# Gated linear attention and feed-forward on one core: the recurrence's result computed transposed in quadrants of 32 columns

## The chip, the core and the metric

The kernel runs on one core of a Trainium2 chip. The metric is the device time of one execution in microseconds (us), as the median of several runs. Times inside an execution come from a profile of one further execution.

## What is computed

The reference chains a gated recurrence over 768 time steps (4 batches, 8 heads, head size 48) with a feed-forward block of 3072 tokens, 384 model columns and 2048 hidden columns. Cut to what matters:

```python
# attention: a complex gate per head and column, capped at magnitude 0.999
mag = np.sqrt(a_re * a_re + a_im * a_im)
scale = np.minimum(mag, 0.999) / (mag + 1e-06)
a_re_n, a_im_n = (a_re * scale, a_im * scale)
for t in range(S):
    S_re, S_im = (ar * S_re - ai * S_im + kv, ar * S_im + ai * S_re)   # kv = outer(k_t, v_t)
    y[:, :, t] = np.einsum('bhd,bhde->bhe', q[:, :, t], S_re)
# feed-forward on x, which is y with the heads side by side: 3072 x 384
h = x @ w_in
sp = np.maximum(h, 0.0) + np.log1p(np.exp(-np.abs(h)))
out = (h * erf(sp)) @ w_out
```

## The kernel before

Two functions stand in the file: `quotient_path`, which runs, and `product_path`, a slower fallback behind a test of value ranges at the end, which this input does not reach. All arithmetic is f32. The weights arrive in 64-bit form and are narrowed to f32 on ScalarE and VectorE in the first units (`narrow`, L676 on).

**Units and chunks.** The tokens are cut into 12 units of 256 tokens, three to a batch; each unit has two chunks (`C = 2`) of 128 tokens. In a chunk all 8 heads are treated. The recurrence is solved by chunks: the gates become cumulated magnitudes `pr` and cumulated angles `CS`, by which q and k are multiplied (`prep`, L835 and L839). That doubles the head size to 96 (cosine and sine side by side). Then, per chunk:

- `cols` (L847, L850) transposes k and q on TensorE, 4 heads to a PSUM tile `tr`, and copies them out as `kT` (ScalarE) and `qT` (VectorE).
- `state` (L870 to L879) forms `kv` = k-transposed times v for each head (96 x 48), adds the state `S` of the chunk before (`Skv`) and multiplies by the gate `w` of the chunk's last row. The first chunk of a batch has no state before it, the last one leaves none behind.
- `scores` (L858, L861) forms the 128 x 128 scores `sc` of each head, keys down the partitions and queries along the columns, and multiplies them by a triangular mask into `A`.
- `y_` (L886, L889, L894): for each head a matmul with `A` as the stationary operand (128 rows, 128 columns) and `v` as the moving one (48 columns), and, unless the chunk is the first of its batch, a second with `qT` as the stationary operand (96 rows, 128 columns) and `S` as the moving one. Both add up in PSUM tile `y`, tokens down the partitions and heads side by side. VectorE copies it to `x`.
- `xT` (L902, L903): three TensorE transposes turn `x` (128 x 384) into the PSUM tile `xt`, model columns down the partitions, and ScalarE copies it into `xT`.

The feed-forward of a unit runs one unit later, out of `xT`: `ff_in` (`hps`, L919, copied to `h` at L921), `softplus` and `erf_times_h` (L645, L948 to L951), and two units later `ff_out` (`ops`, L965).

**What sets the order.** In turn `w` the program makes a list `plan` of steps with due times between 0 and 1: the chunk steps of unit `w` (0.5 for the second chunk, plus the offsets at the end of `chunk`: `y_` at 0.36 and `xT` at 0.45), `ff_in`, `softplus` and `erf_times_h` of unit `w - 1`, `ff_out` of unit `w - 2`, gates of units ahead, the load of q, k and v of unit `w + 1` at 0.62 and of gates of unit `w + 3` at 0.72. The steps are emitted by due time, and the tile layer places the instructions on each engine's queue and adds the waits. [...]

**Buffers and queues.** All loads go through SyncE's queue (`load`, L661). v has two buffers (`bufs=2`), S two, x two. PSUM pool `ps_b` has two banks, shared by `kv`, `y`, `xt` and the gate sums.

An f32 matmul of the program appears in the trace as two MATMUL records, each with a LDWEIGHTS record (its load of the stationary operand) ahead of it: 192 matmuls with `A` (24 chunks of 8 heads) are "x384" there. A transpose of the program is one MATMUL record.

## Time and profile before

| | |
|---|---|
| median of 3 runs | 827.02 us (826.87 to 830.81) |
| the profiled execution | 830.44 us |
| its span, first to last instruction | 828.7 us |
| mean granted TensorE clock | 0.977 |
| TensorE matmuls busy (PE) | 762.6 us |
| TensorE weight loads busy (PEld) | 594.1 us |
| VectorE busy (DVE) | 550.8 us |
| ScalarE busy (ACT) | 602.3 us |

In rows of the profile, L numbers are lines of the kernel before; PE is TensorE's matmuls, PEld its weight loads, DVE VectorE, ACT ScalarE, SPq SyncE's queue of DMA issues. A row such as `y<-v,A 128*128 128x48 f32 x16` names the tiles (written from read), the rows and columns of the array, the moving operand's shape and the count. Rows of the timeline start with the start and the length in us, after merging equal neighbours. A row of groups ends with busy us, mean ns of one, and idle time before them. [...]

### The profile page before, as it was taken

How to read it: one execution, taken by the hardware profiler on the slowest of the kernel's cores; microseconds unless marked ns; L12 is line 12 of the kernel's file. 1: busy time of each engine (PE TensorE's matmuls, PEld its weight loads, DVE VectorE, ACT ScalarE, POOL GpSimd, SP SyncE). 2: the span in 40 equal slices, each digit the busy share in tenths (PEclk: the TensorE clock that was granted, in tenths of full speed). 3: DMA queues.
4: the chain of work that ended last, by engine and by line, in shares of the span. 5: the costliest groups of instructions: out<-in, count | busy, mean ns of one | idle time of the engine just before them, and what ended most of it. 6: DMA issues, size and time to landing. Idle time of an engine off the chain costs nothing.

```text
span 828.7 us, 10183 instructions
## 1 busy us (share of the span) xinstructions
PE 762.6 (92%) x3882; PEld 594.1 (72%) x3882; DVE 550.8 (66%) x875; ACT 602.3 (73%) x787; POOL 1.1 (0%) x8
## 2 busy tenths in 40 slices
PE   2446897999999999999999999999999999999996
PEld 0335695787787777777777787887777787887763
DVE  2799798866964963963973873873874774656262
ACT  7789788878876876876877867867877666566670
POOL 0000000000000000000000000000000000000000
PEclk9998699999999999999999999999999999999998
DMA  8456432211212111221212112113021010000000
GB/s 184 129 183 153 137 112 40 58 39 30 48 39 49 30 39 30 49 40 31 46 39 49 29 39 49 30 38 58 20 39 40 1 38 20 1 1 20 1 19 24
DMA packets 148034, 41.77 MB, mean 50 GB/s; under 512 B 142068, under 2 KB 145160, under 8 KB 147208
## 3 DMA queue, kind: packets, MB, share of 16 engines
q1 hardware_dynamic: 147976, 41.03, 21.7%
q8 instruction: 32, 0.52, 0.3%
q14 instruction: 26, 0.21, 0.1%
HBM read 36.24 MB, written 4.75 MB: 49 GB/s over the span
## 4 chain that ended last, share of the span: by engine, by line
PE 72%; DVE 13%; ACT 10%; issue 2%; DMA 2%; SPq 0%; DVEq 0%; ACTq 0%
PE ops L965 24%; PE hps L919 22%; PE y L886 5%; PE sc L858 5%; PE tr L847 5%; PE y L889 5%; PE kv L870 3%; ACT L644 2%; PE sum L821 2%; PE sum L754 2%; DVE yy L949 2%; DVE e L950 2%; DVE t L948 1%; ACT CS L645 1%; DVE h L951 1%
## 5 line engine op out<-in xcount | busy, mean ns | idle before, releaser
L965 PE MATMUL ops<-w_out_sb,h 128*128 128x384 f32 x768 | 269.0, 495 | 0.5 <-DVE h L951 0.5
L919 PE MATMUL hps<-xT,w_in_sb 128*128 128x256 f32 x1152 | 266.9, 384 | 1.3 <-ACT h L921 0.7
L919 PEld LDWEIGHTS hps<-xT,w_in_sb 128*128 128x128 f32 x1152 | 216.6, 192 | 34.7 <-ACT xT L903 1.0
L965 PEld LDWEIGHTS ops<-w_out_sb,h 128*128 128x128 f32 x768 | 144.5, 194 | 86.7 <-issue 4.8
L921 ACT COPY h<-hps 128x512 f32<-128x512 f32 x96 | 54.6, 580 | 113.5 <-PE hps L919 113.5
L644 ACT ACT_TABLE_LOAD x68 | 87.2, 1283 | 2.0 <-PEq L1063 0.8
L948 DVE TENSOR_TENSOR t<-z,yy 128x512 f32<-128x512 f32 x96 | 65.9, 686 | 23.8 <-ACT yy L645 22.8
L886 PE MATMUL y<-v,A 128*128 128x48 f32 x384 | 71.7, 282 | 5.8 <-DVE A L861 5.8
L645 ACT ACTIVATE e<-z 128x512 f32<-128x512 f32 x96 | 57.4, 626 | 23.1 <-DVE h L951 22.6
L886 PEld LDWEIGHTS y<-v,A 128*128 128x128 f32 x384 | 61.5, 203 | 12.2 <-ACT words L697 5.9
L950 DVE TENSOR_TENSOR e<-e,yy 128x512 f32<-128x512 f32 x96 | 64.4, 686 | 3.5
L949 DVE SCALAR_TENSOR_TENSOR yy<-t,yy 128x512 f32<-128x512 f32 x96 | 65.8, 685 | 0.7
L951 DVE SCALAR_TENSOR_TENSOR h<-e,h 128x512 f32<-128x512 f32 x96 | 64.3, 685 | 0.4
L889 PE MATMUL y<-S,qT 96*128 96x48 f32 x320 | 64.2, 283 | 0.0
L894 DVE COPY x<-y 128x384 f32<-128x384 f32 x24 | 13.4, 557 | 74.2 <-PE y L889 67.8
L858 PE MATMUL sc<-qT,kT 96*128 96x128 f32 x384 | 51.7, 284 | 0.9 <-DVE qT L850 0.9
L858 PEld LDWEIGHTS sc<-qT,kT 96*128 96x128 f32 x384 | 49.4, 197 | 3.6 <-DVE qT L850 1.2
L861 DVE TENSOR_TENSOR A<-sc,triu 128x512 f32<-128x512 f32 x48 | 32.3, 684 | 28.1 <-PE sc L858 28.1
L889 PEld LDWEIGHTS y<-S,qT 96*128 96x128 f32 x320 | 50.8, 199 | 0.0
L645 ACT ACTIVATE yy<-z 128x2048 f32<-128x2048 f32 x24 | 45.9, 1911 | 1.9 <-DVE w_out_sb L700 1.2
L645 ACT ACTIVATE z<-z 128x2048 f32<-128x2048 f32 x24 | 45.9, 1911 | 0.8
L645 ACT ACTIVATE yy<-yy 128x2048 f32<-128x2048 f32 x24 | 45.9, 1912 | 0.7
(80 smaller groups left out, 841.4 us busy)
## 6 DMA issues: line engine op xcount, KB each, us to landing
raw<-in_moe_w_in_dram SPq DMA_DIRECT2D x6, 1024.0 KB, 5.9
raw<-in_moe_w_out_dram SPq DMA_DIRECT2D x8, 768.0 KB, 5.1
ar<-in_a_re_dram SPq DMA_DIRECT2D x24, 192.0 KB, 3.5
ai<-in_a_im_dram SPq DMA_DIRECT2D x24, 192.0 KB, 3.3
q<-in_q_dram SPq DMA_DIRECT2D x24, 192.0 KB, 3.2
k<-in_k_dram SPq DMA_DIRECT2D x24, 192.0 KB, 3.1
v<-in_v_dram SPq DMA_DIRECT2D x24, 192.0 KB, 3.1
out_dram<-o SPq DMA_DIRECT2D x24, 192.0 KB, 1.9
```

Of the source, the lines that this page charges most:

```text
L644: in_order(nc.scalar.preload_act_table_set(sets[0]))
L645: in_order(nc.scalar.activation(func=func, **kw))
L858: nc.tensor.matmul(out=ps[:, j, :], lhsT=st["k", g][0:D2, j, :], rhs=st["q", g][0:D2, j, :], start=True, stop=True)
L886: nc.tensor.matmul(out=y[:, j, :], lhsT=st["A", g][:, i, :], rhs=T["v", u][:, c, j, :], start=True, stop=first)
L889: nc.tensor.matmul(out=y[:, j, :], lhsT=st["q", g][0:D2, i, :], rhs=T["S"][0:D2, j, :], start=False, stop=True)
L919: nc.tensor.matmul(out=ps[:, e, :], lhsT=w_in_sb[:, kd, f0:f0 + P], rhs=T["xT", u][:, kd, :], start=(kd == 0), stop=(kd == KD - 1))
L921: nc.scalar.copy(out=T["h", u, sl][:, i:i + 2, :], in_=ps)
L948: nc.vector.tensor_tensor(out=t, in0=z, in1=y, op=OP.mult)
L949: nc.vector.scalar_tensor_tensor(out=y, in0=t, scalar=-2.0, in1=y, op0=OP.add, op1=OP.mult)
L950: nc.vector.tensor_tensor(out=e, in0=e, in1=y, op=OP.mult)
L951: nc.vector.scalar_tensor_tensor(out=h, in0=e, scalar=1.0 / RT2, in1=h, op0=OP.add, op1=OP.mult)
L965: nc.tensor.matmul(out=ps, lhsT=T["h", u, sl][:, e, jj * P:(jj + 1) * P], rhs=w_out_sb[:, i, :], start=(i == 0), stop=(i == KF - 1))
```

## The change

The matmuls of `y_` swap their operands: `v` and `S` become stationary and `A` and `qT` moving, so that the result comes out with model columns down the partitions, which is what `xT` needs. `y_`, its copy to `x` and the three transposes go; the new `xT` (due at 0.4) runs the matmuls and the ScalarE copy stays.

[...] So the 384 model columns are cut into 12 pieces of 32 (`QUAD`), four to each of the three groups `i` of 128 partitions. Two heads (96 columns) make three pieces: the first lies in the even head, the third in the odd one, and the middle one takes 16 columns of each. v and S are therefore kept in fixed buffers of pairs of heads with 16 zero columns between them (`GAP`): a window of 32 columns that starts at column 32 holds the even head's last 16 and 16 zeros, one that starts at column 48 holds 16 zeros and the odd head's first 16. The middle piece so takes two stationary windows, one of each head, and adds them up. That makes 16 products for a chunk in place of 8, with `A` and again with `qT`: 32 matmuls (16 in the first chunk of a batch) in place of 16 (8). Each has 32 stationary columns instead of 128 and 128 moving columns instead of 48. They are emitted round the four pieces of a group: first product of each, then the second of each, and so on.

Since even and odd heads lie apart in the buffers, each of the two VectorE operations of `state` becomes two on four heads each, and each load of v becomes two. Four small memsets at the start write the zeros.

```diff
@@ -632,6 +632,22 @@
     w_out_sb = const.tile([P, KF, DM], FP, name="w_out_sb")
 
 
+    GAP, QUAD = 16, P // 4
+    PAIR = 2 * D + GAP
+    vbuf = [const.tile([P, C, H // 2, PAIR], FP, name=f"v{i}") for i in range(2)]
+    sbuf = [const.tile([P, H // 2, PAIR], FP, name=f"S{i}") for i in range(2)]
+    for t in vbuf:
+        nc.vector.memset(t[:, :, :, D:D + GAP], 0.0)
+    for t in sbuf:
+        nc.vector.memset(t[:, :, D:D + GAP], 0.0)
+
+    def side(t, e):
+
+        return t[..., e * (D + GAP):e * (D + GAP) + D]
+
     order = mybir.DependencyInfo(mybir.DependencyClass.NoSync, mybir.DependencyReason.DATA)
 
     def act(func, **kw):
@@ -670,7 +686,11 @@
         if 0 <= u < NU:
             load(ldq, "q", q, u)
             load(ldq, "k", k, u)
-            load(ldq, "v", v, u, bufs=2)
+            t = T["v", u] = vbuf[u % 2]
+            for c in range(C):
+                for e in range(2):
+                    src = rows(v, u, c).rearrange("t (h e) d -> e t h d", e=2)[e]
+                    nc.sync.dma_start(out=side(t[:, c], e), in_=src)
 
 
     def narrow(dst, src, shape, i):
@@ -868,43 +888,51 @@
             kv = ps_b.tile([P, H, D], FP, tag="b", name="kv")
             for j in range(H):
                 nc.tensor.matmul(out=kv[0:D2, j, :], lhsT=st["k"][:, j].rearrange("p u d -> p (u d)"),
-                                 rhs=T["v", u][:, c, j, :], start=True, stop=True)
-            ns = att2.tile([P, H, D], FP, tag="S", name="S")
+                                 rhs=side(T["v", u][:, c, j // 2], j % 2), start=True, stop=True)
+            ns = sbuf[(u * C + c) % 2]
             w = T["w", u, c][0:D2].unsqueeze(2).to_broadcast([D2, H, D])
             if first:
-                nc.vector.tensor_tensor(out=ns[0:D2], in0=kv[0:D2], in1=w, op=OP.mult)
+                t = kv
             else:
                 t = att1.tile([P, H, D], FP, tag="part", name="Skv", bufs=2)
-                nc.vector.tensor_tensor(out=t[0:D2], in0=kv[0:D2], in1=T["S"][0:D2], op=OP.add)
-                nc.vector.tensor_tensor(out=ns[0:D2], in0=t[0:D2], in1=w, op=OP.mult)
+                for e in range(2):
+                    nc.vector.tensor_tensor(out=t[0:D2, e::2, :], in0=kv[0:D2, e::2, :], in1=side(T["S"][0:D2], e), op=OP.add)
+            for e in range(2):
+                nc.vector.tensor_tensor(out=side(ns[0:D2], e), in0=t[0:D2, e::2, :], in1=w[:, e::2, :], op=OP.mult)
             st["S"] = ns
 
-        def y_():
-            y = ps_b.tile([P, H, D], FP, tag="b", name="y")
-            for j in range(H):
-                g, i = divmod(j, HG)
-                nc.tensor.matmul(out=y[:, j, :], lhsT=st["A", g][:, i, :], rhs=T["v", u][:, c, j, :],
-                                 start=True, stop=first)
-                if not first:
-                    nc.tensor.matmul(out=y[:, j, :], lhsT=st["q", g][0:D2, i, :], rhs=T["S"][0:D2, j, :],
-                                     start=False, stop=True)
+        def xT():
+
+            if c == 0:
+                T["xT", u] = xp.tile([P, KD, NT], FP, tag="xT", name="xT")
+            ps = ps_b.tile([P, KD, P], FP, tag="b", name="y")
+            for i in range(KD):
+                steps = []
+                for b in range(P // QUAD):
+                    pair, o = divmod((i * P + b * QUAD) // QUAD, 2 * D // QUAD)
+
+                    parts = [(0, o * QUAD)] if o * QUAD < D else []
+                    parts += [(1, o * QUAD + GAP)] if (o + 1) * QUAD > D else []
+                    todo = []
+                    for e, lo in parts:
+                        g, k_ = divmod(2 * pair + e, HG)
+                        todo.append((T["v", u][:, c, pair, lo:lo + QUAD], st["A", g][:, k_, :]))
+                        if not first:
+                            todo.append((T["S"][0:D2, pair, lo:lo + QUAD], st["q", g][0:D2, k_, :]))
+                    steps.append([(b, lhsT, rhs, n == 0, n == len(todo) - 1) for n, (lhsT, rhs) in enumerate(todo)])
+                for n in range(max(map(len, steps))):
+                    for todo in steps:
+                        if n < len(todo):
+                            b, lhsT, rhs, start, stop = todo[n]
+                            nc.tensor.matmul(out=ps[b * QUAD:(b + 1) * QUAD, i, :], lhsT=lhsT, rhs=rhs,
+                                             start=start, stop=stop)
             if not last:
                 T["S"] = st["S"]
-            x = xp.tile([P, DM], FP, tag="x", name="x")
-            nc.vector.tensor_copy(out=x, in_=y.rearrange("p h d -> p (h d)"))
-            st["x"] = x
-
-        def xT():
-            if c == 0:
-                T["xT", u] = xp.tile([P, KD, NT], FP, tag="xT", name="xT")
-            ps = ps_b.tile([P, KD, P], FP, tag="b", name="xt")
-            for i in range(KD):
-                nc.tensor.transpose(out=ps[:, i, :], in_=st["x"][:, i * P:(i + 1) * P], identity=ident)
             nc.scalar.copy(out=T["xT", u][:, :, c * P:(c + 1) * P], in_=ps)
 
         return [(0.0, prep("k", 1)), (0.03, prep("q", 0)), (0.06, cols("k", 0)), (0.09, cols("k", 1)),
                 (0.12, cols("q", 0)), (0.15, cols("q", 1)), (0.2, state), (0.25, scores(0)), (0.28, scores(1)),
-                (0.36, y_), (0.45, xT)]
+                (0.4, xT)]
 
 
     def ff_in(u, sl):
```

On TensorE's queue, here is the second chunk of unit 6 (the first unit of the third batch) in the kernel before, from the middle of its `y` block on:

```order
L889 MATMUL y<-S,qT 128x48
L886 MATMUL y<-v,A 128x48
L889 MATMUL y<-S,qT 128x48
L965 MATMUL ops<-w_out_sb,h 128x384 x4
L902 MATMUL xt<-ident,x 128x128 x3
L965 MATMUL ops<-w_out_sb,h 128x384 x4
L919 MATMUL hps<-xT,w_in_sb 128x256 x12
```

And the same chunk in the changed kernel, its whole block and what follows (v_137 and S_139 are buffers of v and S):

```order
L927 MATMUL y<-A,v_137 32x128 x4
L927 MATMUL y<-qT,S_139 32x128 x4
L927 MATMUL y<-A,v_137 32x128 x2
L927 MATMUL y<-qT,S_139 32x128 x2
L927 MATMUL y<-A,v_137 32x128 x4
L927 MATMUL y<-qT,S_139 32x128 x4
L927 MATMUL y<-A,v_137 32x128
L927 MATMUL y<-qT,S_139 32x128
L993 MATMUL ops<-w_out_sb,h 128x384 x8
L947 MATMUL hps<-xT,w_in_sb 128x256 x12
```

The part of the block ahead of these rows is one more group (x4, x4, x1, x1). In all 24 chunks the block stands in one piece, with nothing between its matmuls; the transposes are gone and the `ops` on both sides of them have closed up.

VectorE's queue around the same chunk before:

```order
L878 TENSOR_TENSOR Skv<-kv,S 96x384
L835 TENSOR_TENSOR kr<-k,pr 128x384
L879 TENSOR_TENSOR S<-Skv,w 96x384
L861 TENSOR_TENSOR A<-sc,triu 128x512 x2
L835 TENSOR_TENSOR qr<-q,pr 128x384
L969 TENSOR_SCALAR o<-ops 128x384
L894 COPY x<-y 128x384
```

And in the changed kernel:

```order
L899 TENSOR_TENSOR Skv<-kv,S_139 96x4x48 x2
L901 TENSOR_TENSOR S_140<-Skv,w 96x4x48 x2
L881 TENSOR_TENSOR A<-sc,triu 128x512 x2
L855 TENSOR_TENSOR kr<-k,pr 128x384
L855 TENSOR_TENSOR qr<-q,pr 128x384
L997 TENSOR_SCALAR o<-ops 128x384
```

Two operations of 384 columns have become four of 192, and the copy to `x` is gone.

## Prediction

> **What bounds the kernel now.** I read the page first, then the busy time by stretches, then who waits on TensorE, then the timeline of one chunk.

> ```profile
> PE 762.6 (92%) x3882; PEld 594.1 (72%) x3882; DVE 550.8 (66%) x875; ACT 602.3 (73%) x787; POOL 1.1 (0%) x8
> ...
> 0.00:150.00 150.00, 94.18 (x449) 74.52 (x449) 115.52 (x169) 122.95 (x174) 1.09 (x8) 0.92 0.50 129
> 150.00:780.00 630.00, 627.68 (x3294) 493.12 (x3294) 411.96 (x661) 458.10 (x591) 0.00 (x0) 0.99 0.17 34
> 780.00:829.00 49.00, 40.69 (x143) 26.45 (x141) 23.30 (x45) 21.25 (x24) 0.00 (x0) 0.95 0.05 18
> ...
> PE sum L754 <- DVE th L751: 18.2, 3, 6.4
> PE sum L821 <- DVE lr L793: 15.9, 1, 15.9
> ```

> The first line is of the page, the next three are stretches (length, then PE, PEld, DVE, ACT and POOL busy, granted clock, DMA), the last two are the longest waits of TensorE. From 150 to 780 us TensorE works for 627.7 of 630 us while VectorE has 218 us to spare and ScalarE 172. There the end moves by what the change adds to or takes from TensorE's stream, and by nothing else. Before 150 us TensorE stands still a third of the time, behind gates and the narrowing of weights, and after 780 us only `ops` is left. The long waits are all of the early stretch.

> **What the old y and its transposes take.** Two timeline pieces of unit 6, its first chunk (16 records of y) and its second (32), with start and length in us:

> ```profile
> 414.40 1.05 PE L858 MATMUL sc<-qT,kT 96*128 96x128 f32 x8
> 415.29 1.46 PE L965 MATMUL ops<-w_out_sb,h 128*128 128x384 f32 x4
> 416.58 1.88 PE L886 MATMUL y<-v,A 128*128 128x48 f32 x16
> 418.30 0.88 PE L754 MATMUL sum<-th,turns 128*128 128x384 f32 x2
> ...
> 440.49 1.48 PE L870 MATMUL kv<-v,kt 128*96 128x48 f32 x16
> 441.81 2.02 PE L858 MATMUL sc<-qT,kT 96*128 96x128 f32 x16
> ...
> 446.24 0.32 PE L886 MATMUL y<-v,A 128*128 128x48 f32 x2
> ...
> 449.75 2.81 PE L965 MATMUL ops<-w_out_sb,h 128*128 128x384 f32 x8
> 452.40 0.49 PE L902 MATMUL xt<-ident,x 128*128 128x128 f32 x3
> 452.72 2.75 PE L965 MATMUL ops<-w_out_sb,h 128*128 128x384 f32 x8
> ...
> 150.00:780.00 630.00, 69.24 (x598) 70.26 (x597) 27.89 (x38) 21.68 (x26) 0.99 0.17 34
> 150.00:780.00 630.00, 10.31 (x63) 8.22 (x63) 9.89 (x21) 0.99 0.17 34
> L886 PE MATMUL y<-v,A x384: 206/275/418, 51.1 to 755.1; 128*128 128x48 f32 x192
> ```

> A full y block runs from 446.24 to 449.75, 3.51 us or 0.110 a record; a first chunk's from 416.58 to 418.30, 1.72 us. Three transposes step by 0.32 us (452.40 to 452.72). Three prices of a record follow. `sc`, 128 moving columns behind 128 stationary ones, steps by (415.29 - 414.40) / 8 = 0.111 us. y moves only 48 columns and still takes 0.110, so its 128 stationary columns set the pace. `kv`, also 48 moving, but 96 stationary columns, steps by (441.81 - 440.49) / 16 = 0.0825 us. By these two a stationary column costs about 0.9 ns, and 32 of them some 26 ns (my estimate from kv and y). The change shrinks the load, but its 128 moving columns cost sc's 0.111.

> The two stretch rows (tile y, then tile xt) count 598 and 63 records in the TensorE-bound stretch. That is 17 full blocks of 32, 3 of 16, the last 6 records of one more, and 21 x 3 transposes. Now: 17 x 3.51 + 3 x 1.72 + 21 x 0.32 = 71.5 us.

> **The new block.** A full chunk has 32 products, so 64 records of 0.111 us. If they run one after another, that is 7.10 us; if all four strips of 32 columns always work at once, each strip has 8 products, 16 records, 1.78 us. No row of this trace shows two matmuls on different strips, so these are the ends. The nearest row, sc, gives the upper one. I take a value between, from two things. Each product is two records on one strip, one behind the other, and TensorE starts matmuls in program order (the timeline's rows stand in the order of its queue). So the second record of a product waits for the first to stream, and the next product, on a free strip, starts together with that second record, not sooner. Two records at a time, 0.111 us a product: 32 x 0.111 = 3.55. Twice a chunk (in the two groups of x4, x4, x1, x1) a product follows another on the same strip, for 0.111 more each: 3.77 us. A first chunk takes 16 x 0.111 = 1.78.

> That strips work side by side at all is my assumption. [...] No run here shows it yet.

> A change from the full array to strips and back, twice a chunk, is not in the trace either. kv and sc, of different widths, follow each other at about their own steps, which speaks for nothing lost; at most the array empties and a full load is exposed, both times. A record of y lasts 0.275 us and steps by 0.110, so emptying costs 0.165; with the load row below (0.192) it is 0.357. Ends: 0 and 0.71 a chunk; I take the middle, 0.33, emptying alone.

> ```profile
> L886 PEld LDWEIGHTS y<-v,A x384: 190/192/337, 50.4 to 755.0; 128*128 128x128 f32 x192
> ```

> [...]

> New: 17 x (3.77 + 0.33) + 3 x (1.78 + 0.33) = 76.0 us, 4.5 more than now. With switches free 69.4 (-2.1), at 0.71 83.6 (+12.1).

> **The early stretch.** In unit 0's second chunk y lies on the chain, at half clock (rows of the chain of waits):

> ```profile
> 78.93 0.63 PE y L886 x2
> ...
> 85.53 0.44 PE y L889 x2
> 86.00 0.57 DVE x L894
> ...
> 86.61 0.92 PE xt L902 x3
> ```

> From the end of y (85.53 + 0.44 = 85.97) to the end of the transposes (86.61 + 0.92 = 87.53) lie 1.56 us of chain, which go; two switches at half clock give back 0.66; y itself, 7.04 us for 32 records (0.22 each, twice the later step), stays by the same count. Unit 1's two chunks gain 2 x (4.10 - 3.83) = 0.5. Together -0.4.

> **The rest.** Edits off TensorE:

> ```profile
> L894 DVE COPY x<-y x24: 556/557/560, 54.6 to 755.6; 128x384 f32<-128x384 f32 x24
> L878 DVE TENSOR_TENSOR Skv<-kv,S x16: 539/554/556, 73.0 to 714.4; 96x384 f32<-96x384 f32 x16
> L839 DVE TENSOR_TENSOR kt<-kr,CS x24: 937/950/959, 30.2 to 715.8; 128x768 f32<-128x768 f32 x24
> L661 SPq DMA_DIRECT2D v<-in_v_dram x24: 368/571/1165, 7.2 to 633.8; - x24
> DMA to landing us min/median/max: 2.6/3.1/4.7
> ...
> 7.63 0.96 DVE L732 TENSOR_TENSOR s<-s,y 128x768 f32<-128x768 f32 x1 [6.62 <-ACT y L640]
> ```

> VectorE loses 24 x 0.557 = 13.4 us. By 0.554 us for 384 columns and 0.950 for 768, an operation has 0.16 fixed; 36 operations split in two (16 `Skv`, 20 `S`) add 5.8. The 7.6 us net count for nothing under TensorE; without that cover they would. The state arrives 0.3 us later, and its use is the next chunk, 30 us on (416.58 to 446.24). v's loads become 48, at most 24 x 0.571 = 13.7 us more of SyncE's queue over the whole span; behind them stand the gates' loads, `w` and the output stores. v lands in 3.1 us and is asked for over a third of a turn ahead (due at 0.62 of a turn of some 60 us), so nothing waits; without that lead each load would cost its 0.6. The zeros' memsets run in the 6.6 us in which VectorE waits for its first input (last row). ScalarE's 24 copies to `xT` stay; the result is ready a transposition earlier, but `hps` uses it a turn later.

> **Sum.** +4.5 - 0.4 = +4.1 on the profiled 830.44. That execution lies 3.4 above the median, which the change should not touch, so against the median 827.02 + 4.1 = **831 us**, 823 to 840 by the switch's ends and 1 us of early slack either way. That is right at the limit of what a measurement of this kernel can tell from no change, 0.5% or 4.1 us.

> **Rivals.**

> *The strips don't overlap.* Then a full block is 64 x 0.111 + 0.33 = 7.43 and a first one 3.88: 17 x 7.43 + 3 x 3.88 = 138.0, +66.4. The early chain pays 64 x 0.22 - 7.04 + 0.66 - 1.56 = 6.1 for the half-clock chunk and about 5 in unit 1 (7.2 less what its idle TensorE absorbs). **904 us**. For it: sc's step is the only one measured at 128 moving columns, and records of this trace overlap only in their tails. Against: strips share no columns and no output partitions. It decides as soon as fewer than two strips work at once.

> *Issue bound.* 64 loads and 64 matmuls a chunk may not be handed out faster than kv's pair, 0.0825 us, the fastest step of the table above: 5.28 + 0.33 = 5.61 a block, 2.97 a first one, 104.3 in all, +32.8 and 3 early: **863 us**. It decides when a pair costs over 0.059 us (3.77 / 64). Against: y's own first two records start 0.04 us apart (0.32 us long as a piece against 0.275 for one), so kv's step is rather its load of 96 columns.

> *All four strips at once.* If a record waiting for its strip doesn't hold up the next strip's, a full block is 1.78 + 0.33 = 2.11 and a first one 0.89 + 0.33 = 1.22: 39.5, -32.0, and early 3.5 + 1.56 - 0.66 = 4.4 from the half-clock chunk and 1 from unit 1: **790 us**; at 0.71 a switch 798. Only TensorE gains, and the other engines have the room quoted above. Against: starts have been in program order everywhere, and each product is two records.

> [...]

> *That it doesn't do what it says* is excluded by the queue's order: 704 products in 24 unbroken blocks, no transposes.

> **How the numbers follow.** Two at a time 0.45, all four 0.27, no overlap 0.18, issue bound 0.10. The range leaves out the 0.18: 788 (all four, 2 below its figure) to 863. The first two hold both signs; the likeliest one's own range is 823 to 840. Of its 0.45, 0.02 is faster by over 0.5% (the low end), 0.22 within and 0.21 slower. Faster: 0.27 + 0.02 = 0.29. Same: 0.22. Slower: 0.21 + 0.18 + 0.10 = 0.49.

> **What would show it.** In the changed profile a full block should run 3.6 to 3.9 us from its first start to its last, with starts in pairs 0.11 us apart; 7.1 us means no overlap, 1.8 to 2.2 all four, 5.3 evenly spaced the issue bound. The gap between the last `ops` start and the first y start, over 0.32, is the switch. TensorE should stay over 99% busy from 150 us on, VectorE's total fall by 6 to 8 us, and no DMA appear among TensorE's waits. A TensorE that waits for VectorE or SyncE in that stretch would prove the whole sum wrong.

## The result and the profile after

The changed kernel takes **789.76 us** (median of 4 runs, 788.12 to 791.46) against 827.44 of the kernel before on the same chip: a ratio of **0.954**, with a 95% interval from 0.950 to 0.957. The forecast was 831 us, some 4 us slower; the kernel became 38 us faster, and the time came out where the rival "all four strips at once" put it (790). The stated range, 788 to 863, holds it only because it was drawn to take that rival in. The profiled execution took 789.87 us, with a span of 788.1.

The page of the changed kernel, the line of busy times and the granted clock in 40 slices:

```profile
PE 722.3 (92%) x4514; PEld 547.5 (69%) x4514; DVE 541.6 (69%) x891; ACT 598.7 (76%) x787; POOL 1.1 (0%) x8
...
PEclk9555798999999999999999999999999999999999
```

Its three stretches, with the columns of the three rows shown of before (length, then PE, PEld, DVE, ACT and POOL busy, granted clock, DMA share, GB/s):

```profile
0.00:150.00 150.00, 93.83 (x568) 70.73 (x569) 118.89 (x182) 125.60 (x179) 1.09 (x8) 0.76 0.52 133
150.00:740.00 590.00, 587.90 (x3807) 450.39 (x3806) 399.43 (x664) 451.88 (x586) 0.00 (x0) 1.00 0.18 36
740.00:789.00 49.00, 40.60 (x143) 26.35 (x141) 23.32 (x45) 21.17 (x24) 0.00 (x0) 0.95 0.05 18
```

TensorE still sets the end in the middle stretch (587.90 of 590 us), and its last part is as long as before, only 40 us earlier. TensorE is handed 632 records more and is busy 40.3 us less. The half clock in the second to fourth slices is the early stretch, where TensorE waits a third of the time; another profiled execution of this kernel has 0.9, 0.9 and 0.7 there and starts its fourth block 0.9 us earlier, so these slices decide little.

The block that the prediction was about, a full one of 64 records, in the timeline of TensorE (start and length in us). I leave out its middle, in which the records of the four strips stand mixed:

```profile
423.06 2.75 PE L993 MATMUL ops<-w_out_sb,h 128*128 128x384 f32 x8
425.74 0.43 PE L927 MATMUL y<-A,v 128*32 128x128 f32 x8
425.98 0.40 PE L927 MATMUL y<-qT,S 96*32 96x128 f32 x8
...
427.56 0.43 PE L927 MATMUL y<-qT,S 96*32 96x128 f32 x4
427.92 5.43 PE L993 MATMUL ops<-w_out_sb,h 128*128 128x384 f32 x16
```

From 425.74 to 427.92 it lasts 2.18 us (3.51 before); the first eight records are through in 0.24 us, where one after another they would take 8 x 0.111 = 0.89. The starts of the first twelve records, out of the trace's records, in ns after the first:

```
  0   6  13  20 | 133 140 146 153 | 242 249 256 262
  first records | second records  | first records of the next
  of 4 products | of the same 4   | product of each strip
```

Four starts stand 7 ns apart, then nothing for 0.11 us, then the next four. My prediction expected pairs.

Where the 40.6 us of span between the two profiled executions came from, by the starts of the same blocks: 2.2 up to the fourth block (146.99 us before, 144.83 after), 6.4 to the seventh (233.29 and 224.74), 29.9 to the last (751.92 and 713.44), 2.1 behind that. In the 29.9, y blocks (from each first start to the next instruction's start) go from 54.5 to 33.7 us and the transposes' 5.6 us go; entering the blocks costs 1.6. Of the 5.2 that are left, 3.4 are the clock (6.8 us at half clock before, none after), which is told with the experiments; the rest is not taken apart.

### The profile page after: what moved, and what is told of

The parts are those of the page before. It is cut to its first block, busy times and chain, and to the rows that moved or that the text cites. A ratio compares the mean times of both kernels' runs of the same rounds, so it can differ in the third digit from the quotient of the medians.

```text
span 788.1 us, 11488 instructions
## 1 busy us (share of the span) xinstructions
PE 722.3 (92%) x4514; PEld 547.5 (69%) x4514; DVE 541.6 (69%) x891; ACT 598.7 (76%) x787; POOL 1.1 (0%) x8
## 4 chain that ended last, share of the span: by engine, by line
PE 71%; ACT 19%; DVE 4%; DMA 2%; issue 2%; SPq 0%; DVEq 0%; ACTq 0%
PE ops L993 26%; PE hps L947 25%; PE tr L867 5%; PE y L927 4%; PE sc L878 4%; ACT L660 3%; PE kv L890 3%; ACT yy L661 3%; ACT z L661 2%; PE sum L774 2%; PE sum L841 2%; DMA raw<-in_moe_w_in_dram 1%; ACT e L661 1%; ACT words L661 1%; ACT CS L661 1%
## 5 line engine op out<-in xcount | busy, mean ns | idle before, releaser
L993 PE MATMUL ops<-w_out_sb,h 128*128 128x384 f32 x768 | 263.9, 491 | 0.0
L993 PEld LDWEIGHTS ops<-w_out_sb,h 128*128 128x128 f32 x768 | 142.3, 191 | 89.0 <-issue 5.2
L661 ACT ACTIVATE e<-z 128x512 f32<-128x512 f32 x96 | 57.9, 627 | 25.1 <-DVE h L979 24.7
L878 PE MATMUL sc<-qT,kT 96*128 96x128 f32 x384 | 53.6, 290 | 1.0 <-DVE qT L870 0.9
L878 PEld LDWEIGHTS sc<-qT,kT 96*128 96x128 f32 x384 | 51.1, 203 | 4.4 <-DVE qT L870 1.9
L927 PE MATMUL y<-A,v 128*32 128x128 f32 x768 | 47.3, 293 | 2.6 <-DVE A L881 2.6
L661 ACT ACTIVATE z<-z 128x2048 f32<-128x2048 f32 x24 | 45.9, 1911 | 0.8
L661 ACT ACTIVATE yy<-z 128x2048 f32<-128x2048 f32 x24 | 45.9, 1911 | 0.7
L661 ACT ACTIVATE yy<-yy 128x2048 f32<-128x2048 f32 x24 | 45.9, 1911 | 0.5
L927 PEld LDWEIGHTS y<-A,v 128*32 128x32 f32 x768 | 34.7, 114 | 16.6 <-issue 10.1
L661 ACT ACTIVATE z<-h 128x2048 f32<-128x2048 f32 x24 | 45.9, 1912 | 0.4
L774 PE MATMUL sum<-th,turns 128*128 128x384 f32 x48 | 23.0, 563 | 21.9 <-DVE th L771 21.4
L927 PE MATMUL y<-qT,S 96*32 96x128 f32 x640 | 41.3, 282 | 0.0
```

Source lines behind the costliest of these rows:

```text
L661: in_order(nc.scalar.activation(func=func, **kw))
L878: nc.tensor.matmul(out=ps[:, j, :], lhsT=st["k", g][0:D2, j, :], rhs=st["q", g][0:D2, j, :], start=True, stop=True)
L927: nc.tensor.matmul(out=ps[b * QUAD:(b + 1) * QUAD, i, :], lhsT=lhsT, rhs=rhs, start=start, stop=stop)
L993: nc.tensor.matmul(out=ps, lhsT=T["h", u, sl][:, e, jj * P:(jj + 1) * P], rhs=w_out_sb[:, i, :], start=(i == 0), stop=(i == KF - 1))
```

## The experiments

My theory after the result: **strips work at once, and a product's second record waits inside its own strip without holding the other strips up.** Rivals: the block is short for another reason (fewer columns to load, whatever the strips do); or strips share a queue that holds some products, so that the order of emission decides; and for the gain as a whole, that part of it is not the block at all.

### The order of the products

*strip by strip*: within a group of 128 columns, all products of a strip, then those of the next.

```
-                for n in range(max(map(len, steps))):
-                    for todo in steps:
-                        if n < len(todo):
-                            b, lhsT, rhs, start, stop = todo[n]
+                for todo in steps:
+                    for b, lhsT, rhs, start, stop in todo:
```

> The changed kernel with the products of a group emitted strip by strip (all two or four records of products of strip 0, then strip 1, and so on) instead of round the strips. Nothing else changes. Theory A (each strip works through its own records, and TensorE looks past a record whose strip is busy): a full block stays at 2.0 to 2.2 us and the time at 786 to 790 us. Theory B (TensorE starts in program order, and four work at once only because the program goes round the strips): only the last record of a strip overlaps the first of the next, 64 - 12 = 52 steps of 0.111 = 5.8 us a full block, 2.9 a first one, 855 to 865 us.

Measured: 794.27 us, ratio 0.961 (0.958 to 0.963).

```profile
427.06 0.42 PE L925 MATMUL y<-A,v 128*32 128x128 f32 x4
...
429.25 0.41 PE L925 MATMUL y<-qT,S 96*32 96x128 f32 x4
429.59 5.43 PE L991 MATMUL ops<-w_out_sb,h 128*128 128x384 f32 x16
```

The block lasts 2.53 us instead of 2.18. So order matters, but with at most four products in a row on one strip it matters little.

*strip by strip over the chunk*: the products of all three groups are collected, then a strip's whole list is emitted, then the next strip's.

```
+            strips = [[] for _ in range(P // QUAD)]
...
+                        strips[b].append((b, i, lhsT, rhs, start, stop))
+            for todo in strips:
+                for b, i, lhsT, rhs, start, stop in todo:
```

> The same, but strip by strip over the whole chunk: all 8 products of strip 0 (16 records with 16 loads), then all of strip 1, and so on. Theory A without a limit to how far TensorE looks ahead: block about 2.0 us, 785 to 790 us. Theory A with a limited view: the fourth strip's first record stands 48 records and 48 loads behind the first; if the view ends before that, fewer strips overlap, 2.7 to 4 us a block, 800 to 825 us. [...] Theory B: 61 steps, 6.8 us, 875 to 885 us.

Measured: 866.2 us, ratio **1.047** (1.045 to 1.050). A full block takes 5.93 us. The timeline's piece of a first chunk, 32 records:

```profile
433.42 2.46 PE L929 MATMUL y<-A,v 128*32 128x128 f32 x32
435.81 2.85 PE L994 MATMUL ops<-w_out_sb,h 128*128 128x384 f32 x8
```

2.39 us instead of 1.03, and its records' starts (ns after the first) show why. Each strip has four products here, eight records. The records do not name their strip; I read it from the program's order and the 0.11 us step that a strip keeps:

```
strip 0:   0 134 | 243 352 | 461 570 | 679 789
strip 1:                     467 600 | 709 819 | 928 1037 | 1146 1255
strip 2:                                         934 1067 | 1176 1285 | ...
```

Strip 1 has nothing to do until then, and yet its first product starts only 6 ns after the *third* of strip 0 does, at 461, as if strip 0's fourth could not leave TensorE's queue sooner, to wait at its strip. That fourth starts at 679, later than strip 1's first, though it stands ahead of it in the program. My reading of these starts: **a strip works on one product and holds one waiting; a further product for the same strip stops the queue for all strips.** I tried this as a counting rule (products leave the queue in program order, 6.5 ns apart; a product occupies its strip for 0.222 us; one waits) against every full block, from the first start to the last, in us:

```
                       one waits   none   two    measured
changed                     1.93   2.37   1.68      1.98
strip by strip              2.23   4.62   1.92      2.33
strip by strip, chunk       5.68   6.35   5.01      5.73
balanced (below)            1.68   1.68   1.68      1.70
halves of 64 (below)        4.11   4.34   3.89      4.19
```

One place fits all five within 0.1 us, none and two don't.

*balanced*: rounds over the strips for the whole chunk, so that no strip is given two products while another has none.

```
-            for todo in strips:
+            for todo in zip(*strips):
```

> Round the strips, but over the whole chunk: the n-th product of each strip's own list of 8, for n from 0 to 7, so that no strip ever waits for the singles of another group. Theory A: the 18 steps of the changed block (1.98 us from first to last start) are 16 plus two of imbalance between strips in the queue's order, so the block falls from 2.18 to 1.9 to 1.95 us, 17 x 0.25 = 4 to 5 us less: 785 us. Rival: the two steps are issue or switch, which the order doesn't change: 789 to 790 us.

The second time with the changed kernel beside it on one chip:

> The changed kernel itself, beside the two kernels that are to be compared with it on one chip. All theories: 789 to 791 us, 0.954 to 0.957 of the kernel before.

> The changed kernel with its products of a chunk in rounds over the four strips, one product a strip each time, again, now beside the changed kernel on the same chip. Theory (a strip holds one waiting product, so the order decides): a full block lasts 1.90 us instead of 2.18, 17 x 0.28 = 4.8 us less TensorE time, of which somewhat over half comes back as waits for VectorE and ScalarE: 787 to 788 us, 2 below the changed kernel. Rival (everything comes back, since another engine now sets the pace between blocks): no difference.

Measured: 787.67 us, ratio 0.952 (0.950 to 0.954). The second time the changed kernel took 788.9 us, ratio 0.955 (0.953 to 0.957), and the balanced one 787.11, ratio 0.952 (0.951 to 0.954).

```profile
425.11 0.42 PE L929 MATMUL y<-A,v 128*32 128x128 f32 x8
...
426.67 0.40 PE L929 MATMUL y<-qT,S 96*32 96x128 f32 x8
427.00 5.43 PE L994 MATMUL ops<-w_out_sb,h 128*128 128x384 f32 x16
```

The block takes 1.90 us, 0.28 less than changed. 17 of them are 4.8 us; the two medians lie 1.8 us apart, and the intervals overlap a little. From the seventh block to the last the y blocks are 4.1 us shorter, the whole stretch only 1.8: the steps of the other matmuls grow by 2.3, since TensorE now meets waits, 1.3 of which the profile names. Those of the changed and of the balanced kernel between 150 and 740 us (total, times, longest):

```profile
PE tr L867 <- DVE kt L859: 1.8, 3, 0.7
PE tr L867 <- ACT kT L870: 0.2, 1, 0.2
```

```profile
PE tr L867 <- DVE kt L859: 2.6, 3, 0.9
PE tr L867 <- ACT kT L870: 0.5, 2, 0.3
PE sum L774 <- DVE th L771: 0.2, 1, 0.2
```

### The strips themselves

*full array*: the same 32 products, each with 128 stationary columns (in the order of *strip by strip*, which I took not to matter without strips).

```
-                        todo.append((T["v", u][:, c, pair, lo:lo + QUAD], st["A", g][:, k_, :]))
+                        todo.append((vw[:, at_:at_ + P], st["A", g][:, k_, :]))
...
-                            nc.tensor.matmul(out=ps[b * QUAD:(b + 1) * QUAD, i, :], lhsT=lhsT, rhs=rhs,
+                        nc.tensor.matmul(out=ps[:, i, :], lhsT=lhsT, rhs=rhs,
```

> Every product takes 128 stationary columns (a wider window of the same buffers) and writes all 128 partitions, so no strips are left; the number of products, their moving columns and everything else stay. The result of the recurrence is left wrong, its size and cost kept. Theory A (the gain comes from strips side by side): 64 records of 0.111, 7.1 us a full block and 3.6 a first one, +4.9 x 17 + 2.5 x 3 = 91 us and some 8 more early: 885 to 900 us, slower than the kernel before. Rival (the gain comes from the transposes, the copy and the shorter chain that went): 790 to 800 us.

Measured: 880.38 us (one run).

```profile
434.74 3.73 PE L928 MATMUL y<-A,v 128*128 128x128 f32 x32
438.31 2.10 PE L994 MATMUL ops<-w_out_sb,h 128*128 128x384 f32 x6
...
465.21 0.38 PE L928 MATMUL y<-A,v 128*128 128x128 f32 x2
...
472.36 3.07 PE L994 MATMUL ops<-w_out_sb,h 128*128 128x384 f32 x9
```

A first chunk takes 3.57 us and a full one (465.21 to 472.36) 7.14, where the prediction's upper end was 7.10. The same count of records takes 1.90 us on four strips, 3.8 times less. The narrow loads alone are not the reason: *strip by strip, chunk* has the same loads and takes 5.93. The block is entered 0.322 us after the last `ops` and left after 0.110, as in the kernel before, so the longer steps around the changed block (below) belong to the change between the full array and strips.

*halves of 64*: two strips of 64 columns.

```
-                        todo.append((T["v", u][:, c, pair, lo:lo + QUAD], st["A", g][:, k_, :]))
+                        todo.append((vw[:, at_:at_ + 2 * QUAD], st["A", g][:, k_, :]))
...
+                for pairs in ((steps[0], steps[2]), (steps[1], steps[3])):
```

> Every product takes 64 stationary columns and one half of the array (output partitions 0 to 63 or 64 to 127), emitted round the two halves. The recurrence's result is left wrong, its cost kept: 32 products a full chunk, 16 on each half. Theory (strips side by side, each doing the two records of a product itself, with room for one waiting product): 32 records of 0.111 on each half, 3.55 us and 0.2 for the way out, 3.7 to 3.8 a full block in place of 2.18, 1.8 to 2.0 a first one; 17 x 1.55 + 3 x 0.85 = 29 us more than the changed kernel, 815 to 820 us. Rival (only division into four helps, or halves don't overlap): 7.1 us, 880 us.

Measured: 828.23 us (one run), a block of 4.39 us: a miss. Two strips with 16 products each would take 32 x 0.111 = 3.55 if both always worked. In the order that I wrote, both lists of a group are of unequal length, so that one half is given several products in a row and the other stands empty. The counting rule gives 4.11 from first to last start for this order; I had not counted it through.

### Entering and leaving

*balanced, cut in two*: rounds 1 to 4 at the block's old place, rounds 5 to 8 (first chunks 1 to 2 and 3 to 4) a little later, behind a piece of the feed-forward part, in most chunks: 19 further visits.

```
-                (0.4, xT)]
+                (0.4, xT_first), (0.47, xT_second)]
```

> The balanced order cut into two blocks of 4 products a strip with other matmuls between, in 19 of 24 chunks: 19 more changes to strips and back. By the steps in the changed kernel's trace (0.416 into a block where 0.322 is usual, 0.200 out of it where 0.111 is) a change there and back costs 0.18 us: 19 x 0.18 = 3.5 us more than the balanced kernel, 790 to 792 us, each piece 1.0 us with its way out. By the 0.33 of the prediction 794 us, with an exposed reload as well (0.71) 801 us; if a cut costs nothing, 788 us.

Measured: 789.59 us (one run, span 787.9).

```profile
424.88 0.43 PE L934 MATMUL y<-A,v 128*32 128x128 f32 x8
...
425.89 2.85 PE L1002 MATMUL ops<-w_out_sb,h 128*128 128x384 f32 x8
428.67 0.43 PE L934 MATMUL y<-A,v 128*32 128x128 f32 x8
...
429.69 2.85 PE L1002 MATMUL ops<-w_out_sb,h 128*128 128x384 f32 x8
```

Two half blocks take 1.01 + 1.02 us where one took 1.90. From the last start ahead of a block (`ops` or a gate sum) to the first y start stand 0.414 to 0.416 us behind 140 us, in every block, cut or not, where 0.322 stood in the kernel before; from the last y start to the next instruction 0.200 instead of 0.111. That is 0.094 + 0.089 = **0.18 us a visit**, and 19 of them 3.5 us. A cut costs 0.05 us more than that, since the strips of each half block start one behind the other and a first step is 0.133 instead of 0.109 us: by the records 19 cuts are 4.4 us. The whole lies just under the expected 790 to 792 us and 1.9 us above the balanced kernel's first time, but by one run and on another chip, so the records' steps carry the price and not this time.

### What the transposes and the moving columns were worth

*before without transposes*: the kernel before, with y copied straight into `xT`.

```
-            x = xp.tile([P, DM], FP, tag="x", name="x")
-            nc.vector.tensor_copy(out=x, in_=y.rearrange("p h d -> p (h d)"))
...
-                nc.tensor.transpose(out=ps[:, i, :], in_=st["x"][:, i * P:(i + 1) * P], identity=ident)
-            nc.scalar.copy(out=T["xT", u][:, :, c * P:(c + 1) * P], in_=ps)
+            nc.scalar.copy(out=T["xT", u][:, :, c * P:(c + 1) * P],
+                           in_=y.rearrange("p h d -> p (h d)").rearrange("p (i t) -> p i t", t=P))
```

> The kernel before without the copy to x and the three transposes: ScalarE copies y into xT as it lies, so what the feed-forward gets is not the transposed result. y's matmuls are untouched. By the sum of the trace before: 21 x 0.32 = 6.7 us of TensorE's bound stretch and 1 to 1.5 early: 818 to 820 us. Rival (the transposes were hidden, or the later copy's wait is what they cost): 826 us; rival on the other side (most of the change's 37 us is here): under 805 us.

Measured: 825.29 us, ratio 0.997 (0.995 to 0.998), only some 2.5 us less: a miss. The transposes are gone from the trace, but TensorE's clock is not the same. Four stretches of this kernel, each behind a y block (a fifth piece follows the block that ends at 148.9 us):

```profile
384.00:388.00 4.00, 4.00 (x11) 2.31 (x11) 0.00 (x0) 3.39 (x5) 0.00 (x0) 0.58 0.49 98
445.00:449.00 4.00, 4.00 (x17) 2.78 (x17) 0.27 (x1) 2.68 (x4) 0.00 (x0) 0.64 0.49 97
568.00:572.00 4.00, 4.00 (x17) 2.88 (x17) 0.00 (x0) 2.62 (x5) 0.00 (x0) 0.62 0.46 91
722.00:726.50 4.50, 4.50 (x14) 2.83 (x14) 1.22 (x2) 3.96 (x5) 0.00 (x0) 0.62 0.00 0
```

TensorE is busy all the time, yet the granted clock (third column from the right) is near a half. Each piece of 3.4 us at half clock loses about 1.7 us. Looking back, the kernel before has such pieces too. A y block of it, the 3.8 us behind it, and the time after that:

```profile
199.00:202.60 3.60, 3.60 (x34) 3.53 (x32) 0.88 (x2) 3.56 (x2) 0.00 (x0) 1.00 0.21 55
202.60:206.40 3.80, 3.80 (x9) 2.13 (x9) 0.56 (x1) 2.73 (x3) 0.00 (x0) 0.55 0.52 104
206.40:210.00 3.60, 3.60 (x14) 2.23 (x14) 2.81 (x5) 2.52 (x4) 0.00 (x0) 1.00 0.35 87
```

It has two more behind the blocks that end at 264.6 and 633.5 us. The changed kernel around the same block has none:

```profile
192.90:195.20 2.30, 2.30 (x66) 2.07 (x65) 0.76 (x2) 2.27 (x2) 0.00 (x0) 1.00 0.27 86
195.20:199.00 3.80, 3.80 (x12) 2.31 (x13) 0.99 (x2) 3.77 (x6) 0.00 (x0) 1.00 0.28 52
```

*before with wide moving*: each y product of the kernel before gets 128 moving columns instead of 48, with the same loads.

```
-                nc.tensor.matmul(out=y[:, j, :], lhsT=st["A", g][:, i, :], rhs=T["v", u][:, c, j, :],
+                nc.tensor.matmul(out=yw[:, lo:lo + P], lhsT=st["A", g][:, i, :], rhs=vw[:, lo:lo + P],
```

> The kernel before with 128 moving columns instead of 48 in each of y's matmuls (a wider window of v and S, written over a wider window of y, so the result is wrong); counts, loads and everything else as before. The 128-column load sets the pace either way, so a block stays at 3.5 to 3.6 us. Theory C (part of the gain: before, the y block keeps the array so little busy that the clock is halved for 3.4 us behind it now and then, three times after 200 us in the profiled execution, 1.7 us each; 128 moving columns keep it busy as in the changed kernel): no half-clock piece behind a y block after 200 us, and 3 to 5 us less than before, 822 to 824 us. Rival (the halved clock has nothing to do with y): 827 us and some half-clock pieces left.

Measured: **819.2 us**, ratio 0.991 (0.989 to 0.993), with a block of 3.57 us, 0.07 longer.

```profile
0.00:150.00 150.00, 97.52 (x476) 78.18 (x477) 120.86 (x178) 128.51 (x181) 1.09 (x8) 0.80 0.53 135
150.00:780.00 630.00, 628.45 (x3317) 494.76 (x3316) 413.48 (x667) 462.07 (x595) 0.00 (x0) 1.00 0.16 33
```

More work, and 8 us faster; behind 132 us no piece at half clock is left while TensorE works. By itself that could be luck, or the order of the instructions: with this edit the tile layer placed some of them otherwise (a y block that `sum` cut in two before, at 176.6 us, is whole here). The trace's clock records leave little room for either. In every profiled execution here the clock changes only on a grid of 3.413 us. I sorted the slots of this grid behind 138 us by how much of each is filled by y's records; TensorE is busy through all of the fullest ones. With 48 moving columns (the two kernels before, with and without transposes) all seven slots with 3.14 us of y or more are followed by half clock, one of the three between 3.0 and 3.1 is, and none of the emptier ones. With 128 moving columns (this run and the next) none of the eleven slots with 3.14 us or more is. So I take a block of 48-column products behind 128-column loads for what lowered the clock in these kernels, when it filled over 3.0 of a slot's 3.413 us; a block of 3.5 us seldom does, hence three pieces for some twenty blocks.

The three pieces are 3 x 1.7 = 5.1 us. What gives the rest of the 8 was not taken apart: of the 12.1 us between the two profiled executions, 6.1 lie ahead of the fourth block (146.99 and 140.90 us), where the order differs too and the mean granted clock of the first 150 us is lower here, 0.80 against 0.92.

*wide moving without transposes*: both edits.

> The kernel before with 128 moving columns in its y products (as in the run of wide moving columns), and without the copy of y and its three transposes: the feed-forward part gets y untransposed, so its values are others. Theory (the transposes are worth their TensorE time of 0.32 us a chunk once the half-clock pieces are gone): 21 x 0.32 = 6.7 us less than the wide kernel's 819.2, and up to 1.5 more from the early chain: 811 to 813 us. Rival (the transposes were worth nothing, because other engines' waits take their place): 818 to 820 us.

Measured: 811.99 us, ratio 0.982 (0.980 to 0.984). Against the wide kernel's 0.991 that is 0.009, about 7.4 us: with the clock steady, the transposes are worth their TensorE time, 21 x 0.32 = 6.7 and something of the early chain.

So the gain can be taken apart in ratios, each against the kernel before: the wide moving columns, for the most part through the clock, 0.009 (1 to 0.991), the transposes 0.009 (to 0.982), the strips 0.027 (to 0.955 of the changed kernel), some 22 us. The order of the instructions differs a little among these kernels, so the parts are rough.

### A further product on strips

*balanced, kv on strips*: each kv product of 96 stationary columns is cut into three of 32.

```
-                nc.tensor.matmul(out=kv[0:D2, j, :], lhsT=st["k"][:, j].rearrange("p u d -> p (u d)"),
-                                 rhs=side(T["v", u][:, c, j // 2], j % 2), start=True, stop=True)
+                for b in range(D2 // QUAD):
+                    nc.tensor.matmul(out=kv[b * QUAD:(b + 1) * QUAD, j, :],
+                                     lhsT=st["k"][:, j].rearrange("p u d -> p (u d)")[:, b * QUAD:(b + 1) * QUAD],
+                                     rhs=side(T["v", u][:, c, j // 2], j % 2), start=True, stop=True)
```

> The balanced order, and each kv product (96 stationary columns, 48 moving) cut into three products of 32 columns on strips 0 to 2; the values are the same. Theory one (strips overlap for any moving width, the step of a strip with 48 moving columns is at most kv's 0.0825 us): a kv block of 16 records goes from 16 x 0.0825 = 1.32 us to 16 x 0.0825 / 2 to 16 x 0.0825, since each strip still has 16 records of which only the load is narrower; if a strip's step falls to 0.04 with the 32-column load it lasts 0.67, plus two switches, 0.18, so 0.4 to 0.5 us less for each of some 18 chunks, 7 to 9 us of TensorE time, of which by the run of the balanced order alone half shows: 783 to 785 us. Rival (a strip's step is set by something else than the loaded columns and stays at 0.08): the block gets longer by the switches, 0.2 us each, and the time is 788 to 792 us.

Measured: **783.26 us**, ratio 0.948 (0.947 to 0.950), the fastest here. The kv block of the balanced kernel, and with kv on strips:

```profile
419.26 1.48 PE L890 MATMUL kv<-v,kt 128*96 128x48 f32 x16
420.57 2.02 PE L878 MATMUL sc<-qT,kT 96*128 96x128 f32 x16
```

```profile
414.80 0.88 PE L891 MATMUL kv<-v,kt 128*32 128x48 f32 x48
415.61 2.05 PE L878 MATMUL sc<-qT,kT 96*128 96x128 f32 x16
```

0.81 us instead of 1.31, less 0.1 to enter. But the gain does not come from there. From the seventh block to the last kv takes 11.3 instead of 18.4 us, and the stretch is only 0.5 us shorter. In the waits of this kernel between 150 and 740 us the time turns up again:

```profile
PE tr L867 <- DVE kt L859: 5.1, 7, 1.0
PE sum L774 <- ACT th L661: 1.8, 2, 0.9
PE tr L867 <- ACT kT L870: 1.0, 4, 0.3
```

They are 7.9 us against the balanced kernel's 3.3. The 3.6 us that the profile shows lie ahead of the fourth block, which starts at 140.9 us instead of 144.5 (the balanced kernel's second profile; 145.1 in its first); which of the early pieces give them was not taken apart, and the granted clock also differs there from one execution to the next.

## Why the prediction was wrong

**What bounds the kernel** held: TensorE, over 99% busy in the middle (587.90 of 590), no DMA among its waits. The long waits are still of the early stretch; the longest:

```profile
PE sum L774 <- DVE th L771: 21.4, 4, 6.8
```

**The block is the step that failed**: "So the second record of a product waits for the first to stream, and the next product, on a free strip, starts together with that second record, not sooner." That made 3.77 us of a full block; it is 2.18, and 1.03 instead of 1.78 in a first chunk. Over 17 and 3 blocks: 17 x 1.59 + 3 x 0.75 = 29.3 us of the 41 between 831 and 789.76. I had read two things out of a trace in which no two matmuls stood side by side in the array: that starts go by program order, and that an f32 product's two records stand in that order one by one. The second record in fact starts 0.133 us after the first and holds no other strip up: the next product starts 7 ns after the first, not 0.11 us. By the counting rule, the queue stops only where a strip would get a third product. Starts by program order did not hold on strips either: in *strip by strip over the chunk*, with its records read as above, the start at 679 ns stands ahead in the program of the one at 467.

**The switch** was over-sized: 0.33 us taken, 0.18 measured. That the array empties twice at a visit was my estimate, out of y's 0.275 us length and 0.110 us step; no run shows it. What the runs show is a first y start 0.094 us later and a next instruction 0.089 us later than in the kernel before. The 2.18 already holds its way out, so block and switch together are 2.28 us instead of 4.10, and 1.13 instead of 2.11 in a first chunk: 17 x 1.82 + 3 x 0.98 = 33.9 us of the 41. The changed records also show what I had only assumed: the switch is paid at both ends of the block.

**The clock** is a term that my sum lacked. I priced y's records by their steps and did not ask why pieces of `ops` behind them were slow. Its three pieces are worth 5.1 us; the run with wide moving columns, which changed the order too, gained 8.

**The transposes** at 0.32 us a chunk were right, once the clock is steady. **The early stretch**: 0.4 us forecast; the fourth block starts 2.2 us earlier in one profiled execution of the changed kernel and 3.1 in another.

**Off TensorE** the steps held. VectorE's total fell by 9.2 us (6 to 8 forecast): the split operations took 0.346 to 0.349 us each where I had 0.358, and neighbours overlap by 78 to 80 ns, so that they add 3.4 us of busy time instead of 5.8. For the v loads, now twice as many, no engine waits:

```profile
L899 DVE TENSOR_TENSOR Skv<-kv,S x32: 343/346/355, 72.5 to 677.6; 96x192 f32<-96x192 f32 x32
L693 SPq DMA_DIRECT2D v<-in_v_dram x48: 368/505/1476, 7.2 to 602.2; - x48
```

**The rivals.** "No overlap" has its price in the full array run (7.14 us a block, 880 us), "issue bound" falls with starts 7 ns apart. "All four strips at once" gave 2.11 with the switch; measured 2.28. Its mechanism was nearly right, but that its 790 is so close is luck, with terms off in opposite directions: the order lost 0.28 us a block, which it did not count, and the early stretch gave 2 to 3 us where it had 5.4; the switch was 0.15 cheaper, and the clock gave back what neither it nor I had seen. Its chance, 0.27, was too small for the one row that spoke against it, and that row was of the full array.

## What to carry to other kernels

Here f32 products with 32 output columns did well on column strips when the program went round the strips, one product for each before the second for any: a full block took 1.90 us so, 5.93 with one strip's whole list after another's, and 7.14 with 128 stationary columns on the full array. By the reading above, the third in a row on one strip stops all. A block of matmuls that moved 48 columns behind loads of 128 cost more than its own time, about 1.7 us in the clock of what came behind it, where half clock followed: compare the granted clock behind such a block before pricing its neighbours. And a rule read from records that all use one resource says nothing of how several of them go.
